# The first batch's start put in an order of its own: gated attention unit and quick-GELU layer

## The chip, the cores and the metric

The kernel runs on one core of a Trainium2 chip. A time is the device time of one execution in microseconds (us), from launch to end; times are medians over several runs. One execution was also taken by the hardware profiler; its span, the time between the first and the last instruction that the profile shows, is a little shorter than its own time. The engines are named as in the profile: PE (TensorE, matmuls), PEld (its weight loads), DVE (VectorE), ACT (ScalarE), POOL (GpSimd) and SP (SyncE, here a queue of transfers).

## The reference

For 8 batches of S = 3008 rows, with u and v of 256 columns and z of 64:

```python
scores = (1.0 / S) * np.matmul(z, z.transpose(0, 2, 1))
attn = np.maximum(scores, 0.0) ** 2
x = u * np.matmul(attn, v)                      # 24064 x 256 over all batches
h = x @ w_in                                    # w_in 256 x 2048
g = h * (1.0 / (1.0 + np.exp(-1.702 * h)))
out = g @ w_out                                 # w_out 2048 x 256
```

The score matrix of a batch is symmetric. Inputs and output are float32; the kernel computes with float16 operands and float32 sums.

## The kernel before, in words

**Tiling.** A batch's 3008 rows are NJ = 24 blocks of 128 (the last one half full), and NCH = 6 chunks of 512 (four blocks each). `ZT` holds z turned: 64 rows, held twice one below the other, and 24 x 128 columns.

**Scores.** `scores(b, group)` makes units (i, jp): the scores of the two key blocks 2jp and 2jp+1 against the 512 queries of chunk i. A unit is two matmuls of 64 rows into a pair of PSUM banks `sc` (two such pairs exist, shared with `hg`), a relu on ACT into `rl` (three buffers, L229), and a square on DVE into `a` (L243). In the first batch a unit of the upper triangle is also turned by a transfer of SP (L249) into `tt`, because the symmetric half of the matrix is not computed but taken from there. In the text, score k, relu k and square k are those of unit (0, k); score k needs the columns of z chunk k // 2.

**Attention.** `attend(b, i)` gives a list of steps; one step is one (or, in two halves, two) matmuls of a block of V by a block of squares into `o`. In the first chunk of the first batch (`both`), step n takes key block n // 2 and column half n % 2, so it needs square n // 4 and V's group n // 8. At the end, DVE multiplies `o` by u, turned before (`turn_u`, L194), into `xt`.

**First batch's z.** In later batches z is turned by a transfer. In the first, `first_z` loads z as float32 into `zf` with SP's queue, `first_cast(g)` casts chunk g twice on DVE (L123, cast g in the text), and `first_zt(g)` turns it: four transposes on PE into `zp` (L129, zp g), and a copy into ZT (L137) by ACT for g = 0 and by DVE for the others (copy ZT g). V is loaded by ACT's queue (first group) and SP's, and cast by POOL in six groups of two casts (L172). `warm_up(n)` issues n matmuls on zeros (L96), whose result is not used.

**Order.** The order of instructions on PE, POOL, SP, DVE and ACT is the program's order, written by hand. Ahead of the loop, z chunks 0 to 2 and units 0 to 2 are handled; in the loop over steps, `FIRST_ZT` says at which step of the first chunk a further z chunk is cast and turned, `SCHED0` at which steps how many units are taken (`take`), and other tables when u is turned and loaded. On DVE a ZT copy and a cast so stand in one queue with the squares. Within `take` all score matmuls of the group come ahead of its relus and squares.

**Up and down.** `up_group(b, q)` makes two blocks of 128 of the 2048 hidden columns for 512 rows: four matmuls into `hg`, the activation on ACT into `gf` (two buffers, L351), a scaling on DVE into `gt` (L352). Groups q = 0 to 7 belong to row chunk 0, 8 to 15 to chunk 1, and so on; groups 0 to 19 are spread over the steps of the last chunk's attention, and from group 20 on each is followed by one `product`. The down projection of the first four chunks is done by seven products P1 to P7 of half the size each, in place of eight; they need sums of blocks of `gt` (`left_sums`, eight DVE operations per chunk, L406 to L414) and four sums of blocks of W2 (`weight_sums`, L385 to L388, once for the whole kernel). The list `SUMS` is a queue of the former: each `up_group` takes one sum from it after its scaling. The latter are issued in the step loop, after up_group 12, 14, 16 and 18 of the first batch.

Of the kernel before, what the change touches and what calls it, by code (L numbers as in the profile page):

```python
# [11 lines left out]
P = 128  # L12
# [3 lines left out]
def kernel(  # L16
# [75 lines left out]
    def warm_up(n):  # L92

        w = ps1.tile([P, CH], F32, name="w", tag="ps1")
        for k in range(n):
            pe.matmul(w, nil[:, :P], nil, start=(k == 0), stop=(k == n - 1))  # L96
# [23 lines left out]
    def first_cast(g):  # L120
        m = g % CB * CB
        for c in range(2):
            dve.tensor_copy(ZT["st"][g // CB][:, m:m + CB, c, :], ZT["f"][g // CB][:, m:m + CB, :])  # L123

    def first_zt(g):
        z2 = ZT["st"][g // CB][:, g % CB * CB:(g % CB + 1) * CB]
        zp = ps1.tile([P, CB, P], F16, name="zp", tag="ps1")
        for k in range(CB):
            pe.transpose(zp[:, k, :], z2[:, k, :, :], ident)  # L129
        zt = ZT[0][:, g * CB:(g + 1) * CB, :].rearrange("d n p -> d (n p)")  # L130
        nb = CB if g < NCH - 1 else CB - 1
        dst = zt[:, :nb * P].rearrange("d (p n) -> d p n", n=nb)
        src = zp[:, :nb, :].rearrange("d n p -> d p n")
        if g == 0:
            act.activation(dst, src, AF.Copy, scale=1.0)
        else:
            dve.tensor_copy(dst, src)  # L137
        if nb < CB:
            dve.tensor_copy(zt[:, nb * P:], zp[:, nb, :])
# [64 lines left out]
    def folded(b, i):  # L204
        return b > 0 and i < NCH - 1

    def scores(b, group):
        scs = []
        zt = ZT[b]
        for i, jp in group:  # L210
            sc = ps2.tile([P, 2, CH], F32, name="sc", tag="ps2")
            turned = b > 0 and i < NCH - 1 and jp >= NU - 2
            kp, qi = (2 * i + jp - (NU - 2), NCH - 1) if turned else (jp, i)
            m = CB // 2 if folded(b, i) and jp == 2 * i + 1 else CB
            for r in range(2):
                h = slice(r * DQK, (r + 1) * DQK)
                pe.matmul(  # L217
                    sc[:, r, :m * P], zt[h, 2 * kp + r, :], zt[h, (qi + 1) * CB - m:(qi + 1) * CB, :],
                    start=True, stop=True,
                )  # L220
            scs.append(sc)
        for (i, jp), sc in zip(group, scs):
            rl = pw.tile([P, 2, CH], F16, name="rl", tag="rl", bufs=3)
            if folded(b, i) and jp == 2 * i + 1:
                rh = rl[:, :, :CH // 2]
                act.activation(rh, sc[:, :, :CH // 2], AF.Relu, scale=csc)
                dve.tensor_tensor(unit[b, i, jp][:, 1], rh, rh, ALU.mult)
                continue
            act.activation(rl, sc, AF.Relu, scale=csc)  # L229
            if folded(b, i) and jp == 2 * i:  # L230
                a = pa.tile([P, CB, 2, P], F16, name="a", tag="a", bufs=21)
                unit[b, i, jp] = a
                r4 = rl.rearrange("p r (q c) -> p r q c", q=CB)
                dve.tensor_tensor(a.rearrange("p q r c -> p r q c"), r4, r4, ALU.mult)
                unit[b, i, jp + 1] = pa.tile([P, 2, 2, CH // 2], F16, name="ad", tag="a", bufs=21)
                sp.dma_start_transpose(
                    unit[b, i, jp + 1][:, 0].rearrange("p g (r c) -> p (g r) c", c=P),
                    a[:, CB // 2:].rearrange("p q r c -> p (q r c)"),
                )
                continue  # L240
            a = pa.tile([P, 2, CH], F16, name="a", tag="a", bufs=21)
            unit[b, i, jp] = a
            dve.tensor_tensor(a, rl, rl, ALU.mult)  # L243
            cj = jp // 2
            if cj > i and (b or cj < NCH - 1):
                if (b, i, cj) not in TT:
                    TT[b, i, cj] = pa.tile([P, CB, CB, P], F16, name="tt", tag="tt", bufs=14)
                k0 = 2 * (jp % 2)
                sp.dma_start_transpose(  # L249
                    TT[b, i, cj][:, k0:k0 + 2].rearrange("p r g c -> p (r g) c"),  # L250
                    a.rearrange("p r c -> p (r c)"),
                )

    def weights(b, i, j):

# [80 lines left out]
    def up_group(b, q):  # L336
        k, fg = divmod(q, NFG)
        i, n = blocks(b)[k]
        hg = ps2.tile([P, FFG, CH], F32, name="hg", tag="ps2")
        for e in range(FFG):  # L340
            ff = fg * FFG + e
            for c in range(NCC):
                pe.matmul(  # L343
                    hg[:, e, :n], W1[:, c, ff * P:(ff + 1) * P], XT[b, i][:, c, :n],
                    start=(c == 0), stop=(c == NCC - 1),
                )
        if fg % 2 == 0:
            GT[b, k, fg // 2] = pa.tile([P, CB, CH], F16, name="gt", tag="tt", bufs=14)
        g = GT[b, k, fg // 2][:, (fg % 2) * FFG:(fg % 2 + 1) * FFG, :n]
        gf = pw.tile([P, FFG, CH], F32, name="gf", tag="gf")  # L350
        act.activation(gf[:, :, :n], hg[:, :, :n], AF.Gelu_apprx_sigmoid, scale=1.0 / FSC)  # L351
        dve.tensor_scalar(g, gf[:, :, :n], FSC, None, ALU.mult)  # L352
        if SUMS:
            SUMS.pop(0)()
        if k < NST and fg == NFG - 1:
            SUMS.extend(left_sums(b, k))

# [35 lines left out]
    def left_sums(b, k):  # L395
        out_ = []
        for name in ("S1", "S2", "S3", "S4"):
            for h in range(2):
                out_.append(lambda name=name, h=h: left_sum(b, k, name, h))
        return out_  # L400
# [172 lines left out]
    LOADW = {(3, NJ + 1): 0, (3, NJ + 11): 1, (4, 2): 2, (4, 10): 3, (5, 0): 4, (5, 6): 5, (5, 12): 6, (5, 18): 7}  # L573
    LOAD = {(3, NJ + 4): 4, (4, NJ + 5): 5}

    FIRST_ZT = {3: 3, 11: 4, 19: NCH - 1}
    SCHED0 = {
        0: {0: 1, 6: 2, 14: 2, 22: 2, 30: 2, 38: 2},
        1: {0: 2, 8: 2, 15: 2, 22: 2, 30: 2, 38: 2},
# [6 lines left out]
    queue = []  # L586

    def take(b, n):
        if n:
            group = [queue.pop(0) for _ in range(n)]  # L590
            scores(b, group)

    def fill(b):
        assert not queue
# [7 lines left out]
    warm_up(7)  # L602
    first_cast(0)
    first_zt(0)
    warm_up(3)
    first_cast(1)
    take(0, 2)
    first_zt(1)
    warm_up(2)
    take(0, 1)  # L610
    load_u(0, 1)
    first_cast(2)
    first_zt(2)

    for b in range(B):
        nup = NCH * NFG
        sched, turn, load = (SCHED, TURN, LOAD) if b else (SCHED0, TURN0, LOAD0)
        head = 0
        for i in range(NCH):
            for n, step in enumerate(attend(b, i, b == 0 and i < 2)):  # L620
                if b == 0 and i == 0 and n == 5:
                    load_u(0, 0)
                if b == 0 and i == 0 and n in FIRST_ZT:
                    first_cast(FIRST_ZT[n])
                    first_zt(FIRST_ZT[n])
                if (i, n) in turn:
                    turn_u(b, turn[i, n])
                if (i, n) in load:
                    load_u(b, load[i, n])
                if b == 0 and (i, n) in LOADW:  # L630
                    load_w(LOADW[i, n])
                take(b, sched[i].get(n, 0))
                if i == NCH - 1 and n >= HEAD and (n - HEAD) * LAGY // (2 * NJ - 2 - HEAD) >= head and head < LAGY:
                    up_group(b, head)
                    head += 1
                    if b == 0 and head in (13, 15, 17, 19):
                        weight_sums()[head // 2 - 6]()
                step()
        more = b + 1 < B
        if more:  # L640
            for i in range(2):
                load_u(b + 1, i)
            load_z(b + 1)
            for n0 in range(0, NJ, VB):
                load_v(b + 1, n0, sp)
            fill(b + 1)
        downs, prods = down_list(b), products()
        for q in range(head, nup):
            if more and q in (head + 14, head + 20):
                k = int(q == head + 20)  # L650
                turn_u(b + 1, k)
                load_u(b + 1, k + 2)
            up_group(b, q)
            product(b, *prods.pop(0))
        if more:
            while downs[0][0] < NCH - 2:
                down(b, *downs.pop(0))
            for k in range(NCH - 2, NCH):
                turns, steps = down64(b, k)
                at = {n: 3 - len(turns) for n in turns} | TAIL[len(turns)]  # L660
                for n, step in enumerate(steps):
                    take(b + 1, at.get(n, 0))
                    step()
        else:
            for d in downs:
                down(b, *d)
# [30 lines left out]
```

## Time and profile before

| | |
|---|---|
| median of 8 runs | 1219.36 us (1217.9 to 1220.97) |
| the profiled execution, its own time | 1218.1 us |
| its span | 1216.3 us |
| mean granted PE clock | 0.995 of full |
| PE waits for the z cast (four times) | 5.9 us |
| PE waits for the ZT copy (once) | 2.3 us |
| last V cast of the first batch ends | 17.33 us |
| score 10 (step 30 of the first chunk) starts | 29.84 us |

A row of the timeline has the start, the busy time, the engine, the line and operation, the output and the inputs with their shapes, the count, and in brackets how long the engine was idle before it and what released it. A row of the waits says who waited for whom: the total, the number of times, the longest. Rows by stretches give for each engine the busy time and the number of instructions, then the granted clock of PE as a share of full speed, the share of the DMA engines that was busy, and GB/s. Idle time of an engine that is not the bottleneck costs nothing by itself.

### The profile page before, as it was taken

What the parts mean: (1) busy time and instruction counts of PE and PEld (TensorE: products, weight loads), DVE (VectorE), ACT (ScalarE), POOL (GpSimd) and SP (SyncE); (2) the same over time, 40 slices, a digit from 0 to 9 for tenths busy, and PEclk for the clock granted to TensorE, in tenths of its full rate; (3) what the DMA queues carried; (4) which work ended last, traced back from release to release, by engine and by line L of the source; (5) the groups of instructions that cost most, each with busy time, mean ns of one, the idle gap of its engine ahead of it and who ended that gap; (6) DMA issues with size and microseconds to landing.
All of it is one profiled execution on the core that took longest, in us unless ns stands there. A gap on an engine that the chain in (4) does not pass through costs nothing.

```text
span 1216.3 us, 28032 instructions
## 1 busy us (share of the span) xinstructions
PE 1197.5 (98%) x11692; PEld 715.7 (59%) x11692; DVE 817.7 (67%) x1257; ACT 768.6 (63%) x897; POOL 306.6 (25%) x361
## 2 busy tenths in 40 slices
PE   6999999999999999999999999999999999999998
PEld 2345775557744676446764467554775547844576
DVE  4769956498554985459754697547966489564882
ACT  3777675476744768457684576836677366772763
POOL 3244410354003530034200461004520134101000
PEclk8999999999999999999999999999999999999999
DMA  9884479554794638946299553984449764496012
GB/s 216 139 137 59 156 153 168 105 114 124 144 162 99 121 110 166 152 88 154 72 174 163 87 140 92 182 145 77 135 111 184 133 85 149 116 175 116 1 36 70
DMA packets 366111, 152.32 MB, mean 125 GB/s; under 512 B 313248, under 2 KB 358048, under 8 KB 365984
## 3 DMA queue, kind: packets, MB, share of 16 engines
q1 hardware_dynamic: 328960, 113.16, 48.5%
q0 software_dynamic: 35392, 35.80, 14.6%
q8 instruction: 91, 1.49, 0.5%
q10 hardware_dynamic: 1632, 1.57, 0.4%
q14 instruction: 36, 0.29, 0.1%
HBM read 60.29 MB, written 24.64 MB: 70 GB/s over the span
## 4 chain that ended last, share of the span: by engine, by line
PE 95%; DVE 2%; DMA 2%; ACT 1%; issue 0%; ACTq 0%
PE o L302 38%; PE hg L343 26%; PE st L439 16%; PE yp L518 8%; PE sc L217 6%; DMA tt<-a 2%; PE yp L473 1%; ACT rl L229 1%; DVE gt L352 1%; PE w L96 0%; DVE a L243 0%; PE zp L129 0%; DVE s L410 0%; ACT gf L351 0%; DVE zst L123 0%
## 5 line engine op out<-in xcount | busy, mean ns | idle before, releaser
L351 ACT ACTIVATE gf<-hg 128x1024 f32<-128x1024 f32 (+1 forms) x384 | 385.6, 1007 | 167.3 <-PE hg L343 139.3
L229 ACT ACTIVATE rl<-sc 128x1024 f16<-128x1024 f32 x311 | 308.1, 1025 | 218.9 <-PE sc L217 217.0
L302 PEld LDWEIGHTS <-V 64*128 64x128 f16 (+1 forms) x4052 | 233.9, 95 | 254.1 <-issue 12.8
L343 PE MATMUL hg<-xt,W 128*128 128x512 f16 (+1 forms) x1408 | 354.6, 374 | 0.8 <-ACT gf L351 0.8
L352 DVE TENSOR_SCALAR gt<-gf 128x1024 f16<-128x1024 f32 (+1 forms) x384 | 275.4, 718 | 94.2 <-ACT gf L351 91.1
L243 DVE TENSOR_TENSOR a<-rl 128x1024 f16<-128x1024 f16 x276 | 190.8, 692 | 193.9 <-ACT rl L229 193.3
L302 PE MATMUL o<-a,V 64*128 64x512 f16 (+2 forms) x2010 | 318.2, 373 | 0.0
L187 POOL DMA_DIRECT2D uq<-in_u_dram x188 | 129.6, 696 | 519.3 <-PE sc L217 345.2
L302 PE MATMUL o<-tt,V 64*128 64x512 f16 (+1 forms) x1762 | 215.5, 376 | 3.3 <-DMA tt<-a 3.1
L343 PEld LDWEIGHTS <-W 128*128 128x128 f16 x1536 | 141.1, 98 | 118.7 <-issue 1.6
L439 PEld LDWEIGHTS <-gt 128*128 128x128 f16 x2048 | 125.1, 98 | 28.5
L217 PE MATMUL sc<-ZT 64*128 64x512 f16 (+1 forms) x692 | 122.2, 370 | 2.6 <-DVE ZT L137 2.3
L439 PEld LDWEIGHTS <-s 128*128 128x128 f16 x1536 | 93.8, 98 | 21.4 <-issue 0.6
L172 POOL CAST V<-vst 128x512 f16<-128x512 f32 x96 | 88.0, 954 | 66.9 <-DMA vst<-in_v_dram 66.8
L518 PE MATMUL yp<-W,gt 64*128 64x256 f16 x1664 | 104.0, 270 | 0.0
L518 PEld LDWEIGHTS <-gt 64*128 64x128 f16 x1664 | 80.6, 94 | 19.1 <-POOLq L84 4.1
L319 DVE TENSOR_TENSOR xt<-o,ut 128x512 f16<-128x512 f32 x80 | 51.5, 685 | 38.1 <-PE o L302 38.1
L439 PE MATMUL st<-WT,s 128*128 128x128 f16 x1024 | 67.6, 219 | 0.3 <-ACT uP L449 0.3
L439 PE MATMUL st<-WT,gt 128*128 128x128 f16 x1024 | 67.6, 219 | 0.0
L439 PE MATMUL st<-W,gt 128*128 128x128 f16 x1024 | 67.6, 219 | 0.0
L217 PEld LDWEIGHTS <-ZT 64*128 64x128 f16 x692 | 37.6, 94 | 39.8 <-issue 8.1
L152 POOL COPY zst<-zst 128x768 f16<-128x768 f16 x14 | 44.6, 3188 | 54.6 <-DMA zst<-in_z_dram 54.6
(49 smaller groups left out, 636.1 us busy)
## 6 DMA issues: line engine op xcount, KB each, us to landing
vst<-in_v_dram SPq DMA_DIRECT2D x39, 512.0 KB, 5.1
uq<-in_u_dram POOLq DMA_DIRECT2D x156, 128.0 KB, 3.3
out_dram<-y SPq DMA_DIRECT2D x32, 512.0 KB, 3.7
tt<-a SPq DMA_TRANSPOSE x230, 3.5
uq<-in_u_dram POOLq DMA_DIRECT2D x32, 112.0 KB, 3.0
out_dram<-y POOLq DMA_DIRECT2D x7, 512.0 KB, 5.1
vst<-in_v_dram SPq DMA_DIRECT2D x8, 384.0 KB, 4.7
out_dram<-y POOLq DMA_DIRECT2D x7, 384.0 KB, 5.0
```

The costliest lines, as they stand in the source:

```text
L172: pool.tensor_copy(V16[b][:, n0:n0 + VB, k, :].rearrange("p n (q c) -> p n q c", c=QW), vst.rearrange("p n (q k c) -> p n q k c", k=NCC, c ...
L187: eng.dma_start(uq[k * QW:(k + 1) * QW, :n // QW].rearrange("t q k c -> t q (k c)"), src[:, :, cs])
L217: pe.matmul(sc[:, r, :m * P], zt[h, 2 * kp + r, :], zt[h, (qi + 1) * CB - m:(qi + 1) * CB, :], start=True, stop=True,)
L229: act.activation(rl, sc, AF.Relu, scale=csc)
L243: dve.tensor_tensor(a, rl, rl, ALU.mult)
L302: ins = pe.matmul(acc[c][:, :n], V16[b][h, j, c, :], weights(b, i, j)[h], start=(k, m) == first[c], stop=(k, m) == final[c],)
L319: dve.tensor_tensor(x[:, c, :n], acc[c][:, :n], ut[:, :n], ALU.mult)
L343: pe.matmul(hg[:, e, :n], W1[:, c, ff * P:(ff + 1) * P], XT[b, i][:, c, :n], start=(c == 0), stop=(c == NCC - 1),)
L351: act.activation(gf[:, :, :n], hg[:, :, :n], AF.Gelu_apprx_sigmoid, scale=1.0 / FSC)
L352: dve.tensor_scalar(g, gf[:, :, :n], FSC, None, ALU.mult)
L439: pe.matmul(bank[:, m, :], lhs()[:, f, m, :], right[:, ff, :], start=name in ("P1", "P2", "P5") and m == 0 and ff == 0, stop=ff == NFF // ...
L518: ins = pe.matmul(yp[s // per][:, s % per, :], GT[b, k, ff // CB][h, ff % CB, s * P:(s + 1) * P], W2[h, ff, :], start=new, stop=n == last[ ...
```

## The change

- `scores` is split: it issues the score matmuls and returns one function per unit, `square`, which issues the unit's relu, square and transfer. `take` calls all of them at once, as before.
- Ahead of the loop, the matmuls of units 0 and 1 are issued, then z chunk 1 is turned, then unit 0's relu and square, the cast of chunk 2, unit 1's relu and square, and unit 2. Before, both units were complete ahead of the turn of chunk 1, and the cast and turn of chunk 2 came behind unit 2.
- The second `warm_up` has two matmuls in place of three, and the third one (two matmuls) is gone.
- Chunk 2 is now turned in the loop. The steps of the turns are 2, 7, 13 and 21 in place of (ahead of the loop), 3, 11 and 19. At each of them the turn now comes first, and behind it the cast of the next chunk.
- The four sums of W2 are appended to `SUMS` behind the eight sums of chunk 0, in place of their own places in the step loop. They are so taken by up_group 16 to 19, and the sums of each later chunk four groups later than before.

```diff
-        for (i, jp), sc in zip(group, scs):
-            rl = pw.tile([P, 2, CH], F16, name="rl", tag="rl", bufs=3)
...
+        return [lambda u_=u_, sc=sc: square(b, *u_, sc) for u_, sc in zip(group, scs)]
+
+    def square(b, i, jp, sc):
+        rl = pw.tile([P, 2, CH], F16, name="rl", tag="rl", bufs=3)
...
         if k < NST and fg == NFG - 1:
-            SUMS.extend(left_sums(b, k))
+            SUMS.extend(left_sums(b, k) + (weight_sums() if b == k == 0 else []))
...
-    FIRST_ZT = {3: 3, 11: 4, 19: NCH - 1}
+    FIRST_ZT = {2: 2, 7: 3, 13: 4, 21: NCH - 1}
...
     def take(b, n):
-        if n:
-            group = [queue.pop(0) for _ in range(n)]
-            scores(b, group)
+        for post_ in scores(b, [queue.pop(0) for _ in range(n)]):
+            post_()
...
     warm_up(7)
     first_cast(0)
     first_zt(0)
-    warm_up(3)
+    warm_up(2)
     first_cast(1)
-    take(0, 2)
+    posts = scores(0, [queue.pop(0) for _ in range(2)])
     first_zt(1)
-    warm_up(2)
+    posts[0]()
+    first_cast(2)
+    posts[1]()
     take(0, 1)
     load_u(0, 1)
-    first_cast(2)
-    first_zt(2)
...
                 if b == 0 and i == 0 and n in FIRST_ZT:
-                    first_cast(FIRST_ZT[n])
                     first_zt(FIRST_ZT[n])
+                    if FIRST_ZT[n] + 1 < NCH:
+                        first_cast(FIRST_ZT[n] + 1)
...
                     up_group(b, head)
                     head += 1
-                    if b == 0 and head in (13, 15, 17, 19):
-                        weight_sums()[head // 2 - 6]()
                 step()
```

The body of `square` is that of the old loop in `scores`, with `return` for `continue`.

More of the change, by code (lines that the diff above doesn't have):

```diff
@@ L221, in scores @@
             scs.append(sc)
-        for (i, jp), sc in zip(group, scs):
-            rl = pw.tile([P, 2, CH], F16, name="rl", tag="rl", bufs=3)
[L224 to L241, printed above, removed]
-            unit[b, i, jp] = a
[L243 to L252, printed above, removed]
@@ new lines, in scores @@
+        return [lambda u_=u_, sc=sc: square(b, *u_, sc) for u_, sc in zip(group, scs)]
+    def square(b, i, jp, sc):
+        rl = pw.tile([P, 2, CH], F16, name="rl", tag="rl", bufs=3)
+        if folded(b, i) and jp == 2 * i + 1:
+            rh = rl[:, :, :CH // 2]
+            act.activation(rh, sc[:, :, :CH // 2], AF.Relu, scale=csc)
+            dve.tensor_tensor(unit[b, i, jp][:, 1], rh, rh, ALU.mult)
+            return
+        act.activation(rl, sc, AF.Relu, scale=csc)
+        if folded(b, i) and jp == 2 * i:
+            a = pa.tile([P, CB, 2, P], F16, name="a", tag="a", bufs=21)
+            unit[b, i, jp] = a
+            r4 = rl.rearrange("p r (q c) -> p r q c", q=CB)
+            dve.tensor_tensor(a.rearrange("p q r c -> p r q c"), r4, r4, ALU.mult)
+            unit[b, i, jp + 1] = pa.tile([P, 2, 2, CH // 2], F16, name="ad", tag="a", bufs=21)
+            sp.dma_start_transpose(
+                unit[b, i, jp + 1][:, 0].rearrange("p g (r c) -> p (g r) c", c=P),
+                a[:, CB // 2:].rearrange("p q r c -> p (q r c)"),
+            )
+            return
+        a = pa.tile([P, 2, CH], F16, name="a", tag="a", bufs=21)
+        unit[b, i, jp] = a
+        dve.tensor_tensor(a, rl, rl, ALU.mult)
+        cj = jp // 2
+        if cj > i and (b or cj < NCH - 1):
+            if (b, i, cj) not in TT:
+                TT[b, i, cj] = pa.tile([P, CB, CB, P], F16, name="tt", tag="tt", bufs=14)
+            k0 = 2 * (jp % 2)
+            sp.dma_start_transpose(
+                TT[b, i, cj][:, k0:k0 + 2].rearrange("p r g c -> p (r g) c"),
+                a.rearrange("p r c -> p (r c)"),
+            )
```

## The prediction

> **What bounds the kernel now.** I read the busy times first, then TensorE's waits, then the timeline of the two places where it waits.
>
> ```profile
> PE 1197.5 (98%) x11692; PEld 715.7 (59%) x11692; DVE 817.7 (67%) x1257; ACT 768.6 (63%) x897; POOL 306.6 (25%) x361
> PEclk8999999999999999999999999999999999999999
> ```
>
> TensorE is the bound; no other engine is over 67%. Only the first slice (30 us) has a low clock. So an edit pays only where TensorE is idle or at half clock, and TensorE's own waits over the whole run are short:
>
> ```profile
> PE zp L129 <- DVE zst L123: 5.9, 4, 2.3
> PE o L302 <- DMA tt<-a: 3.1, 4, 1.4
> PE sc L217 <- DVE ZT L137: 2.3, 1, 2.3
> PE hg L343 <- ACT gf L351: 0.8, 2, 0.4
> PE st L439 <- ACT uP L449: 0.3, 1, 0.3
> ```
>
> Rows 1 and 3 (8.2 us, the three columns being total, times, longest) lie before 27 us, rows 4 and 5 between 106 and 117 us; both are places that the diff touches. Row 2 lies in later batches and is not touched. Next, the clock by stretches of 3.41 us (columns: busy time and count of PE, PEld, DVE, ACT, POOL; granted clock; DMA share; GB/s):
>
> ```profile
> 6.75:10.16 3.41, 1.11 (x10) 0.43 (x8) 1.99 (x3) 1.93 (x2) 0.89 (x2) 1.00 0.97 323
> 10.16:13.57 3.41, 1.13 (x8) 0.45 (x6) 1.16 (x4) 1.02 (x1) 2.33 (x5) 0.50 1.09 352
> 13.57:16.99 3.42, 2.50 (x10) 0.84 (x9) 1.82 (x4) 1.02 (x1) 2.33 (x5) 0.50 0.91 161
> 16.99:20.40 3.41, 3.41 (x10) 0.71 (x9) 1.21 (x2) 1.57 (x2) 2.99 (x5) 0.50 0.98 181
> 23.81:27.22 3.41, 1.64 (x12) 0.63 (x9) 2.09 (x5) 1.49 (x2) 0.00 (x0) 1.00 1.20 189
> ```
>
> The clock was full in 6.75 to 10.16, halved for the next 10.24 us, and full from 20.40 on. A stretch in which PE was busy 33% lost it, one of 48% kept it, one of 73% did not win it back, one of 100% did. At half clock a 512-column matmul takes 0.43 us, else 0.2155. The timeline shows how one turn of z waits:
>
> ```profile
> 10.65 1.02 ACT L229 ACTIVATE rl<-sc 128x1024 f16<-128x1024 f32 x1 [1.97 <-PE sc L217]
> 11.71 0.72 DVE L243 TENSOR_TENSOR a<-rl 128x1024 f16<-128x1024 f16 x1 [1.71 <-ACT rl L229]
> 12.36 0.48 DVE L123 CAST zst<-zf 128x256 f16<-128x256 f32 x2
> 12.90 0.61 PE L129 MATMUL zp<-ident,zst 128*128 128x128 f16 x4 [2.28 <-DVE zst L123]
> 13.54 0.69 DVE L137 COPY ZT<-zp 128x512 f16<-128x512 f16 x1 [0.70 <-PE zp L129]
> ```
>
> VectorE is a strict queue and idle for 1.71 us; the cast, whose z landed by about 7 us (issued by 2.6 us, 4.3 us to land), stands behind a square that waits for ScalarE, and TensorE waits 2.28 us for it. This repeats for every turn.
>
> **Part 1, the first batch's order.** I carry the queues forward in the new order, each start being the end of the one ahead or of its inputs plus 0.05 us, with these durations: four transposes or a score pair 0.2155 at full and 0.43 at half clock, ScalarE's relu 1.02 (0.91 from start to start), square 0.69 (0.60), ZT copy 0.68, two casts 0.48. Done for the old order, this puts score 10 (step 30 of the first chunk) at 29.2; the trace has 29.84, so the method is 0.6 short in 25.5.
>
> New order: zp0 at 4.4, two warm-ups instead of three to 5.7, scores 0 and 1 from 5.7, zp1 at 6.7 once cast 1 ends at 6.6. Copy ZT1 now stands ahead of square 0 and runs 7.3 to 8.0 (before 9.32 to 10.0), so score 2 starts at 8.05 instead of 10.06, score 3 at 8.3 when relu 1 frees its bank pair. Square 0 ends at 8.6: steps 0 and 1; cast 2 stands between squares 0 and 1, so zp2 at 9.1, steps 2 to 5 to 10.2. Copy ZT2 is now queued behind squares 2 and 3, which wait for relu 3 (ends 10.4): ZT2 ends 11.75, score 4 at 11.8, TensorE idle 1.6 us. Scores 4 and 5, step 6, zp3, steps 7 to 12 run to 13.95; zp4 waits for cast 4 behind squares 4 and 5 and ZT3, to 15.9, idle 1.95. From there nothing waits until score 10 at 20.9. Against 29.2 this is **8.4 us earlier**. It splits into idle time 9.3 to 5.2 (4.1), three warm-ups dropped (0.43 + 2 x 0.215 = 0.9), and 15 matmuls' worth of work at full instead of half clock (15 x 0.215 = 3.2), with 0.1 of rounding. A range for this part: 5.7 (clock lost as before) to 9.6 (before's clock stretches falling worse than in this profile).
>
> The clock decides 2.6 us of this, and dropped warm-ups speak against the change. By the rows: in my timetable PE's share of the stretches to 10.16, 13.57, 16.99 and 20.40 is 67, 53, 43 and 100% without the pipeline tails that the trace counts as busy; the old stretch to 27.22, traced at 48%, is 41% in that count, so each lies above one that kept its clock, the third barely. The Trainium skill (TensorE: Matmul & The Clock Gate, "What's actually happening") says that the clock halves after at least one idle window of about 3.4 us; the 33% stretch here lost it with no gap over 2.3 us, so row and rule differ and the row decides. By the rule nothing is lost, 8.4; if the stretch at 43% loses it, the next runs at half clock, 1.7 less.
>
> Queues past which things move: SP and POOL keep their order, only times change. SP's first two transposes go at 10.4 and 11.2 instead of 12.46 and about 16, and the four loads of u chunk 0 at about 12.5 instead of 17.21, now beside V's loads, whose last cast ended at 17.33. V's last group is needed at step 40, about 23.6, so it has 6 us, and the groups before it 4 or more. u chunk 1 is issued by POOL at 17.3 after V's casts and is turned at step 28 of the next chunk (before 44.75, then about 36.4). Transposes of squares 2 and 3 are needed at about 26.7. Nothing else has a start of its own, so the whole gain should travel to the end.
>
> Squares and casts now fall on POOL's ten V casts (0.61 each, 9.27 to 17.33). The Trainium skill (SBUF — State Buffer, "Who interferes with whom") says that a VectorE operation with two SBUF inputs shares a read interface with GpSimd, and whoever issued first holds it for a whole instruction. The rows below show both sides: a sum of 1.31 instead of 0.68 beside a copy on POOL, and a copy of 6.85 instead of 1.01 beside a full VectorE.
>
> ```profile
> 103.45 1.31 DVE L412 TENSOR_TENSOR s<-s,gt 128x1024 f16<-128x1024 f16 x1
> 111.00 6.85 POOL L152 COPY zst<-zst 128x768 f16<-128x768 f16 x1 [4.63 <-DMA zst<-in_z_dram]
> ```
>
> By the rule one holder at a time costs VectorE 0.1 us net, which my timetable holds. By the 6.85 row, V's second group, cast at 9.27, would not end before VectorE pauses at 12.4 or so; step 8 wants it at 12.9, and zp4 would slip by 1 us or less. I take the rule, and keep 1 to 3 us for the range, since a late cast comes again with each group.
>
> **Part 2, the sums of W2.** Four 0.60 us sums leave groups 12, 14, 16 and 18 and join the queue at groups 16 to 19, where they push the second block's sums four groups back.
>
> ```profile
> 105.66 0.67 DVE L406 TENSOR_TENSOR gt<-gt 128x1024 f16<-128x1024 f16 x1
> 106.26 0.68 DVE L385 TENSOR_TENSOR WT<-W 128x1024 f16<-128x1024 f16 x1
> 106.86 0.68 DVE L352 TENSOR_SCALAR gt<-gf 128x1024 f16<-128x1024 f32 x1
> 107.63 1.02 ACT L351 ACTIVATE gf<-hg 128x1024 f32<-128x1024 f32 x1 [0.77 <-DVE gt L352]
> 108.70 1.02 PE L343 MATMUL hg<-xt,W 128*128 128x512 f16 x4 [0.40 <-ACT gf L351]
> ```
>
> VectorE is full from 98.5 to 120: gt frees gf for ScalarE, whose gf frees hg's banks for TensorE. A group is 1.24 to 1.43 us on TensorE and 1.2 on VectorE with one sum, but 1.8 with two. Counted between matmul starts, TensorE loses 0.25 (106.9), 0.55 (108.7), 0.53 (111.7) and 0.44 (116.2) = 1.77 us. With one sum a group, the first stays (it comes from the slow rows at 103 to 105), the others go: gt 13 starts 0.6 earlier, and the first P6 starts at 114.67 instead of 116.20. **1.5 us**, from 0 to 1.8. The moved sums lie beside products of 1.755 us a group: groups 40 to 43, empty before, take the last four. The first consumers keep slack: P6 of block 0 is in group 21 with its W sum in 17, P6 of block 1 in group 28 with S2 in 22 and 23. Without that cover it would cost 0.6 us a sum, 2.4 in all.
>
> **Sum.** 8.4 + 1.5 = 9.9. The profiled execution took 1218.1 (span 1216.3), which gives 1208.2; the median of the runs is 1219.36, 1.3 above it, which gives **1209.5**.
>
> **Rivals.** (a) TensorE stays at half clock from 10.16 to 20.40 as before, for want of warm-ups: 2.6 us lost, 1212.1. For it: no stretch there is over 67%; against: 48% kept it. (b) VectorE and POOL hold each other up, V's groups come late: 3 us lost, 1212.5. The 6.85 row speaks for it, the undelayed casts at 124.75 (8 in 8.0 us) against. (c) Part 2 gives nothing, because POOL's copies keep VectorE late: 1211.0. (d) The saved time meets a load of fixed start (u chunk 1) and comes back whole: 1219.4; the 9 us of slack above speak against. (e) **Slower**: the clock stays half past the prologue. Every us of it costs 0.5; after (a)'s 2.6 it must last until about 40 us to eat 9.9 and 2.4 more, with PE full for six stretches, though one full stretch restored it at 20.40. About 1222.
>
> **How the numbers follow.** Likeliest 0.62, (a) 0.15, (b) 0.12, (c) 0.04, (d) 0.02, (e) 0.05. 0.2% is 2.4 us, about what a measurement can tell from no change. Faster: 0.93, same 0.02, slower 0.05. The likeliest one's own range is 1207 to 1211; to hold 8 in 10 it goes to 1214, past (a) to (c) and their sums of two.
>
> **What would show it.** Right: waits of zp on casts 4 in number before, about 2 us in one or two places after; score 10 near 21.5 (20.9 and the 0.6 that the method falls short); clock 1.00 from 6.75 on; ZT2 starting right behind square 3; no wait of hg on gf past 107 (less 8.4) and P6 with no wait on uP. Wrong: half clock after 10 us, V casts of over 1 us each, o waiting for V, or a later stage that grew between 30 and 97 us.

## The result, and the profile after

The changed kernel takes 1210.7 us (median of 11 runs, 1207.84 to 1212.22), the kernel before, in the same rounds, 1219.27 us (32 runs, 1215.54 to 1224.92). The ratio is 0.9926, with a 95% interval of 0.9916 to 0.9937: about 9 us less. The forecast was 1209.5, within 1207.0 to 1214.0. The profiled execution took 1210.7 us, its span is 1208.9 us (before 1216.3).

Busy times and granted clock by slices, changed kernel:

```profile
PE 1193.8 (99%) x11689; PEld 716.9 (59%) x11689; DVE 818.9 (68%) x1257; ACT 768.4 (64%) x897; POOL 304.6 (25%) x361
PEclk9999999999999999999999999999999999999999
```

TensorE's waits over the whole run, changed kernel (left out is the first matmul's wait for its zeros, 1.2 us as before):

```profile
PE o L304 <- DMA tt<-a: 5.0, 5, 2.0
PE sc L217 <- DVE ZT L137: 2.7, 2, 1.9
...
PE zp L129 <- DVE zst L123: 1.1, 2, 0.8
```

The waits on cast and copy of z fell from 8.2 to 3.8 us, those of hg and P6 are gone; the wait on transposes, in later batches, is 5.0 instead of 3.1. The clock by its own stretches, same kernel (the boundaries lie elsewhere than in the profile of before):

```profile
5.86:9.28 3.42, 2.34 (x19) 0.96 (x16) 2.93 (x7) 2.97 (x4) 0.57 (x1) 1.00 0.91 276
9.28:12.69 3.41, 1.47 (x10) 0.36 (x7) 3.41 (x6) 1.05 (x2) 3.41 (x5) 1.00 1.09 356
12.69:16.10 3.41, 3.36 (x13) 1.21 (x11) 2.83 (x5) 1.79 (x2) 3.33 (x5) 0.50 1.20 285
```

One stretch at half clock is left of three. It follows a stretch in which PE was busy 43%. Next, the turns of chunks 2, 3 and 4 in the timeline of the changed kernel:

```profile
8.68 2.77 DVE L245 TENSOR_TENSOR a<-rl 128x1024 f16<-128x1024 f16 x3
11.38 0.68 DVE L137 COPY ZT<-zp 128x512 f16<-128x512 f16 x1
11.98 1.27 DVE L123 CAST zst<-zf 128x256 f16<-128x256 f32 x2
12.11 0.61 PE L217 MATMUL sc<-ZT 64*128 64x512 f16 x4 [1.94 <-DVE ZT L137]
15.83 1.26 DVE L123 CAST zst<-zf 128x256 f16<-128x256 f32 x2
17.15 0.40 PE L129 MATMUL zp<-ident,zst 128*128 128x128 f16 x4 [0.80 <-DVE zst L123]
22.66 0.61 PE L217 MATMUL sc<-ZT 64*128 64x512 f16 x4
```

The same marks in the kernel before: score 10, the first up_group's matmul, and the first product with a sum of W2 (P6):

```profile
29.84 0.61 PE L217 MATMUL sc<-ZT 64*128 64x512 f16 x4
86.03 1.03 PE L343 MATMUL hg<-xt,W 128*128 128x512 f16 x4
116.20 1.05 PE L439 MATMUL st<-WT,s 128*128 128x128 f16 x16 [0.28 <-ACT uP L449]
```

In the changed kernel score 10 starts 7.18 us earlier, and the first up_group's matmul 7.17 (78.86 against 86.03): what the start of the batch (the prologue, up to score 10) had won arrives there whole. The pairs of casts of chunks 3 and 4 take 1.27 and 1.26 us, not 0.48. In the groups that follow, the changed kernel's timeline has:

```profile
98.65 1.02 ACT L353 ACTIVATE gf<-hg 128x1024 f32<-128x1024 f32 x1 [1.00 <-DVE gt L354]
99.73 1.02 PE L345 MATMUL hg<-xt,W 128*128 128x512 f16 x4
100.97 1.03 PE L345 MATMUL hg<-xt,W 128*128 128x512 f16 x4
107.50 1.06 PE L441 MATMUL st<-WT,s 128*128 128x128 f16 x16
```

The first stall stays (99.73 behind gf), then the groups follow each other every 1.24 or 1.43 us until the products join them. The first P6 (last row) is 28.64 us behind the first up_group; before it was 116.20 - 86.03 = 30.17. So the second part gave 1.53 us.

### The profile page after: what moved, and what is told of

Same layout as the page of the kernel before. It is cut to its first block, busy times and chain, and to the rows that moved or that the text cites. A ratio compares the mean times of both kernels' runs of the same rounds, so it can differ in the third digit from the quotient of the medians.

```text
span 1208.9 us, 28025 instructions
## 1 busy us (share of the span) xinstructions
PE 1193.8 (99%) x11689; PEld 716.9 (59%) x11689; DVE 818.9 (68%) x1257; ACT 768.4 (64%) x897; POOL 304.6 (25%) x361
## 4 chain that ended last, share of the span: by engine, by line
PE 95%; DMA 2%; DVE 1%; ACT 1%; issue 0%; SPq 0%; ACTq 0%
PE o L304 37%; PE hg L345 26%; PE st L441 17%; PE yp L520 8%; PE sc L217 6%; DMA tt<-a 2%; PE yp L475 1%; ACT rl L231 0%; DVE a L245 0%; DMA zf<-in_z_dram 0%; DVE gt L354 0%; DVE zst L123 0%; ACT gf L353 0%; DVE ZT L137 0%; DVE s L414 0%
## 5 line engine op out<-in xcount | busy, mean ns | idle before, releaser
L217 PEld LDWEIGHTS <-ZT 64*128 64x128 f16 x692 | 37.7, 94 | 39.2 <-issue 7.1
L194 DVE STREAM_TRANSPOSE ut<-uq 128x1024 f32<-128x1024 f32 (+1 forms) x48 | 58.3, 1215 | 0.0
```

The source lines that it names most:

```text
L194: dve.transpose(ut[:, :, :n // QW, :].rearrange("p k q t -> p q k t"), UQ.pop((b, i))[:, :n // QW])
L217: pe.matmul(sc[:, r, :m * P], zt[h, 2 * kp + r, :], zt[h, (qi + 1) * CB - m:(qi + 1) * CB, :], start=True, stop=True,)
```

## The experiments

All marks are starts on TensorE in one profile of each kernel, in us. "hg" is the first up_group, "P6" the first product with a sum of W2, "yp" the first matmul behind batch 0's products. "Waits on tt" are TensorE's waits for transposed units over the whole run. The ratio is to the kernel before in the same rounds, from 6 to 32 runs on a side.

| kernel | score 10 | hg | P6 | yp | waits on tt | span | ratio (95%) |
|---|---|---|---|---|---|---|---|
| before | 29.84 | 86.03 | 116.20 | 161.16 | 3.1 | 1216.3 | |
| changed | 22.66 | 78.86 | 107.50 | 152.46 | 5.0 | 1208.9 | 0.9926 (0.9916 to 0.9937) |
| p1_only | 22.16 | 78.36 | 108.53 | 153.49 | 2.0 | 1206.8 | 0.9953 (0.9935 to 0.9972) |
| p2_only | 29.89 | 86.09 | 114.73 | 159.68 | 4.9 | 1216.2 | 0.9993 (0.9981 to 1.0004) |
| after_warm | 24.27 | 80.46 | 109.11 | 154.06 | 1.6 | 1207.0 | 0.9933 (0.9917 to 0.9950) |
| zcast_act | 20.85 | 77.04 | 105.69 | 150.64 | 3.8 | 1206.3 | 0.9924 (0.9906 to 0.9942) |
| after_again | 24.39 | 80.58 | 109.23 | 154.19 | 3.8 | 1209.2 | 0.9919 (0.9904 to 0.9935) |
| after_third | 22.25 | 78.44 | 107.09 | 152.04 | 3.1 | 1206.6 | 0.9921 (0.9905 to 0.9937) |
| before_fill | 28.69 | 84.89 | | 160.01 | 2.6 | 1213.6 | 0.9975 (0.9967 to 0.9983) |
| hold_posts | 20.54 | 76.73 | 105.38 | 150.33 | 4.3 | 1206.3 | 0.9902 (0.9887 to 0.9917) |
| hold_posts_2 | 20.70 | 78.39 | | 151.99 | 4.1 | 1207.0 | 0.9911 (0.9890 to 0.9931) |
| hold_zact | 18.24 | | | 164.29 | 16.7 | 1218.7 | 0.9936 (0.9912 to 0.9960) |
| hold_zact_2 | 18.27 | 80.09 | | 153.69 | 8.5 | 1209.8 | one run |

### Each part alone

p1_only is the changed kernel with the sums of W2 in their old places:

```diff
-            SUMS.extend(left_sums(b, k) + (weight_sums() if b == k == 0 else []))
+            SUMS.extend(left_sums(b, k))
...
                     head += 1
+                    if b == 0 and head in (13, 15, 17, 19):
+                        weight_sums()[head // 2 - 6]()
```

> Only the new order of the prologue; the sums of W2 stay in their old places. Theory: the two parts add. Score 10 (step 30 of the first chunk) starts at about 22.7 us as in the changed kernel, 7.2 us before the old one, and TensorE still loses about 1.5 us between groups 15 and 21 (hg waiting for gf twice, P6 once). Time 7.2 us below the kernel before, 1212. Rival, that the prologue's gain is worth more in the median than in one profile: 8 us or more below, 1211 or less.

p2_only is the kernel before with the opposite edit at those two places.

> The old prologue; only the four sums of W2 join the queue of the block sums. Theory: from the first up_group to the first P6 TensorE takes 1.5 us less than before, nothing comes back in groups 20 to 47, time 1.5 us below the kernel before, 1217.8. Rival, that the later sums give it back beside GpSimd's casts: the first P6 is 1.5 us earlier but the end of batch 0's products (first yp) is not, time unchanged.

TensorE's waits in p1_only, of which the last two rows are those between groups 15 and 21:

```profile
PE hg L345 <- ACT gf L353: 0.8, 2, 0.4
PE st L441 <- ACT uP L451: 0.3, 1, 0.3
```

P6 of p2_only in the timeline:

```profile
114.73 1.06 PE L439 MATMUL st<-WT,s 128*128 128x128 f16 x16
```

From hg to P6, p1_only takes 108.53 - 78.36 = 30.17 us, as before, and p2_only 114.73 - 86.09 = 28.64, as the changed kernel: the sums are the whole of that difference, and the prologue has no share in it. From P6 to yp all four take 44.95 to 44.96 us, so nothing comes back in the groups that took the moved sums: p2_only's rival is ruled out. In the time, part 1 alone is 5.7 us below the kernel before (3.4 to 7.9), which holds the 7.2 expected and just not the rival's 8; part 2 alone is 0.9993 with an interval across 1, so its 1.5 us is shown by the profiles, not by the times. At yp, 7.67 (p1_only) and 1.48 (p2_only) are 9.15; the changed kernel has 8.70, with a score 10 that was 0.5 later in this profile. So the parts add, as near as single profiles can tell.

### The warm-ups

```diff
-    warm_up(2)
+    warm_up(3)
     first_cast(1)
...
     first_zt(1)
+    warm_up(2)
     posts[0]()
```

> The changed kernel with the warm-ups of before put back (three ahead of the cast of chunk 1, two behind the turn of chunk 1). As the prediction counted them, three warm-ups are worth 0.9 us: score 10 at 23.5, time 0.9 above the changed kernel. Rival: the first score pair is not on the path (the z transfer, cast 1 and zp1 are), so score 10 moves by 0.3 us or less and the time by as much; if the extra work keeps the clock full from 12.7 to 16.1 us, zp4 still waits for its cast, and nothing is gained by it.

after_warm puts the three warm-ups back. The time is 0.9933, with the changed kernel's 0.9919 to 0.9926 inside its interval; that interval is 4 us wide, so the times alone do not exclude 0.9 us. zp4 starts at 17.12, where three profiles of the changed kernel have 16.74, 17.15 and 17.24. So up to there the warm-ups cost nothing beyond this scatter: zp1 waits for cast 1 with or without them. Score 10 is at 24.27, but for another reason, which these stretches of after_warm show:

```profile
14.64:18.05 3.41, 1.08 (x10) 0.40 (x9) 2.83 (x5) 0.05 (x1) 3.21 (x5) 1.00 1.23 209
18.05:21.47 3.42, 3.42 (x14) 1.26 (x10) 1.98 (x5) 1.94 (x2) 2.14 (x4) 0.50 1.23 170
```

The wait ahead of zp4 left PE busy 32% of a stretch, and the next one, full of work, ran at half clock. In the changed kernel's first profile the half-clock stretch (12.69 to 16.10) ended before zp4, so its slow matmuls only shortened that wait.

### The changed kernel again

> The changed kernel once more, for its scatter beside the runs of this call. Theory: what follows the first yp is 1051.3 to 1052.1 us plus TensorE's waits on tt (1.6 to 5.0 us in six profiles, with or without the change), so the 1.9 us more that the changed kernel's profile waited there are chance; this profile has 1.6 to 5 us of them and the first yp at 152 to 153. Rival: the earlier start brings later transposes into collision: 5 us or more again.

> The changed kernel a third time: ratio to the kernel before 0.9919 to 0.9926 as in the two calls before; first yp between 152.4 and 154.2 us, by whether the clock's halved stretch falls under a wait or under full work.

These are two more measurements of the changed kernel, without an edit. The ratios are 0.9919 and 0.9921. The first yp came at 154.19 and 152.04 us, a little outside what was expected both times. The stretches of after_again around its two losses of the clock:

```profile
4.58:7.99 3.41, 1.78 (x16) 0.63 (x15) 1.87 (x4) 2.54 (x3) 1.23 (x2) 1.00 0.82 258
7.99:11.40 3.41, 3.41 (x14) 1.21 (x12) 3.31 (x6) 1.94 (x2) 2.06 (x3) 0.50 1.07 364
14.82:18.23 3.41, 1.22 (x11) 0.40 (x9) 2.92 (x5) 0.01 (x1) 3.41 (x6) 1.00 1.16 233
18.23:21.64 3.41, 3.41 (x12) 1.33 (x11) 1.93 (x5) 1.93 (x2) 1.46 (x3) 0.50 1.41 186
```

Here it lost the clock twice, after stretches with PE busy 52% and 36%; in after_third not at all after the start (score 10 at 22.25). The 52% lies above the 48% that kept the clock in the kernel before, so the busy share of a stretch alone does not decide. Between the three profiles of one program score 10 differs by 2.1 us. From zp4 to score 10, after_again takes 7.15 us and after_third 5.51: these 1.6 us are the half-clock stretch under full work. The other 0.5 lies ahead of zp4, where the copy ZT2 starts at 11.44 against 10.96, behind three squares that ended at 11.51 against 11.04.

The waits on tt: in thirteen profiles, the span behind yp, less the waits on tt that lie behind yp, is 1051.0 to 1052.2 us. For the kernel before it is 1216.33 - 161.16 - 3.1 = 1052.1, for the changed one 1208.93 - 152.46 - 5.0 = 1051.5, for after_third 1206.63 - 152.04 - 3.1 = 1051.5. So behind yp it is these waits that differ from profile to profile, and they are no larger with the change: three profiles of the same kernel had 5.0, 3.8 and 3.1, before and p2_only, with the old prologue, 3.1 and 4.9. The rival of after_again's expectation (5 us or more again) did not come.

### The clock alone

```diff
     first_zt(1)
-    warm_up(2)
+    warm_up(8)
     take(0, 1)
     load_u(0, 1)
     first_cast(2)
+    warm_up(8)
     first_zt(2)
...
                     first_cast(FIRST_ZT[n])
+                    warm_up(3)
                     first_zt(FIRST_ZT[n])
```

> The kernel before, with TensorE's idle stretches in the prologue filled with matmuls on zeros: eight in place of two behind the turn of chunk 1, eight ahead of the turn of chunk 2, three ahead of each of the later turns. It measures the clock alone. Theory: the clock stays full from the first 7 us on, and the 15 matmuls' worth of work at half clock, counted at 3.2 us in the prediction, is worth less because part of it lies ahead of waits: score 10 at about 28.1 instead of 29.84, 1.7 us. Rival: the whole 3.2, score 10 at 26.6; or nothing, if the waits swallow all of it.

before_fill is the kernel before with idle TensorE time filled. Its wait for the casts, and score 10 in its timeline:

```profile
PE zp L129 <- DVE zst L123: 4.4, 4, 1.3
```

```profile
28.69 0.61 PE L217 MATMUL sc<-ZT 64*128 64x512 f16 x4
```

The clock is full from 5.87 us to the end, and score 10 moves by 1.15 us: neither 3.2 nor nothing, and below the 1.7 expected. Four waits on the cast remain, 4.4 us, though filled in part with zeros. In the time the ratio is 0.9975 (0.9967 to 0.9983), 2.1 to 4.0 us, more than the 1.15 at score 10. The spans of the two profiles differ by 2.7; 0.5 of that is shorter waits on tt, and about 1 lies in the rest behind yp. What makes it is open. A worse clock in other executions of the kernel before does not explain it: in these rounds their mean granted clocks are 0.994 to 0.996, and the profiled execution has 0.995.

Two profiles with a full clock from the first 6 us on compare the two orders alone: before_fill has score 10 at 28.69, after_third at 22.25, so the new order is worth 6.4 us there (with the dropped warm-ups, for which after_warm shows nothing). So of the change's 7 us in the prologue the clock is a small part; the order of the queues is the rest.

### What still delays the turns: casts beside GpSimd

```diff
-            dve.tensor_copy(ZT["st"][g // CB][:, m:m + CB, c, :], ZT["f"][g // CB][:, m:m + CB, :])
+            dst, src = ZT["st"][g // CB][:, m:m + CB, c, :], ZT["f"][g // CB][:, m:m + CB, :]
+            if g < 3:
+                dve.tensor_copy(dst, src)
+            else:
+                act.activation(dst, src, AF.Copy, scale=1.0)
```

> The changed kernel with the casts of z chunks 3, 4 and 5 on ScalarE, in the same places of the order. If the missing 1.2 us of the prologue came from those casts waiting on VectorE for GpSimd's casts of V (1.27 instead of 0.48 us a pair), zp4 starts about 0.8 to 1.2 us earlier than 17.15 and score 10 at 21.5 to 21.9, time about 1 us below the changed kernel. Rival, that the squares ahead set zp4's time: zp4 at 16.9 or later, time as the changed kernel.

The timeline of zcast_act:

```profile
14.29 1.33 ACT L127 ACTIVATE zst<-zf 128x256 f16<-128x256 f32 x4
15.06 0.40 PE L133 MATMUL zp<-ident,zst 128*128 128x128 f16 x4 [0.59 <-ACT zst L127]
20.85 0.60 PE L221 MATMUL sc<-ZT 64*128 64x512 f16 x4
```

zp4 starts 2.1 us earlier and score 10 1.8 us earlier than in the changed kernel's first profile, more than expected. But the clock differs too: here it was full from 4.05 us on. Against after_third, which also had a full clock, zp4 is 1.7 and score 10 1.4 us earlier. Two things go at once: ScalarE's casts take 0.72 us beside GpSimd's, and they stand behind relu 5 instead of behind square 5 and copy ZT3. So this run shows that the cast's place on VectorE set zp4's time, and does not divide it between the two. Other profiles of the same prologue don't divide it either: in p1_only the casts of chunk 4 took 0.48 us, but squares 4 and 5 ended 0.3 us later (15.59 against 15.30), and zp4 started at 16.66; in after_third the casts took 1.27 us, and zp4 started at 16.74. In the time zcast_act (0.9924) can't be told from the changed kernel.

### The next step of the same idea

hold_posts holds relu and square of units 2 and 3 back behind ZT2 and cast 3, and those of 4 and 5 behind ZT3 and cast 4:

```diff
     posts[1]()
-    take(0, 1)
+    held = scores(0, [queue.pop(0)])
...
                     if FIRST_ZT[n] + 1 < NCH:
                         first_cast(FIRST_ZT[n] + 1)
+                    while held:
+                        held.pop(0)()
...
-                take(b, sched[i].get(n, 0))
+                if b == 0 and i == 0 and n in (0, 6):
+                    held.extend(scores(0, [queue.pop(0) for _ in range(sched[i][n])]))
+                else:
+                    take(b, sched[i].get(n, 0))
```

> The changed kernel with relu and square of units 2 and 3 held back behind the copy of ZT2 and the cast of chunk 3, and those of units 4 and 5 behind ZT3 and the cast of chunk 4. If the order on VectorE (ZT2 behind two squares that wait for ScalarE) is what still stops TensorE, score 4 starts at about 10.3 instead of 12.11, zp4 at about 13.2 instead of 17.15, score 10 at about 18.5 instead of 22.66: 4 us below the changed kernel. Rival: V's casts then set the pace (group 1 at step 8, group 2 at step 16), 1 to 2 us.

> hold_posts once more, beside the changed kernel in the same call. Theory: it is about 2 us below the changed kernel, as its first yp at 150.33 against 152.46 to 154.19 says; ratio to the kernel before about 0.990 against 0.992. Rival: the two agree within 0.5 us, because the transposes of the first batch, issued closer together, cost it back in some executions.

The timeline of hold_posts:

```profile
9.26 0.68 DVE L137 COPY ZT<-zp 128x512 f16<-128x512 f16 x1
10.00 0.61 PE L217 MATMUL sc<-ZT 64*128 64x512 f16 x4
12.90 1.26 DVE L123 CAST zst<-zf 128x256 f16<-128x256 f32 x2
14.22 0.40 PE L129 MATMUL zp<-ident,zst 128*128 128x128 f16 x4 [1.42 <-DVE zst L123]
20.54 0.61 PE L217 MATMUL sc<-ZT 64*128 64x512 f16 x4
```

ZT2 and score 4 start 2.1 us earlier than in the changed kernel's first profile, with no wait of score 4 left; zp4 starts 2.9 us earlier, and score 10 2.1, half of what was expected. Against after_third, with a full clock on both sides, score 10 is 1.7 earlier. The cast of chunk 4 is slow again (1.26). The ratios are 0.9902 and 0.9911, where the changed kernel in the same rounds has 0.9919 and 0.9921: medians of 1207.87 against 1209.41, and 1208.06 against 1209.99, so 1.5 and 1.9 us less. The intervals overlap, but both measurements agree in sign and with the 1.7 to 2.1 us of the profiles. It has the lowest ratio of all kernels here.

hold_zact is hold_posts with zcast_act's edit as well.

> As hold_posts, with the casts of z chunks 3, 4 and 5 on ScalarE too. Theory that VectorE is still the pace: another 0.5 to 1 us, score 10 at about 17.7. Rival: ScalarE is now as full as VectorE and the casts stand ahead of relus there: same as hold_posts within 0.3, or later.

> hold_zact once more for its profile. Theory: the wait of 13.7 us on a transpose at 39 us was no accident of one execution; the transposes of the first batch follow each other faster there and land late, so TensorE waits again for tt before 60 us, 3 us or more. Rival: an accident; no wait on tt before 60 us and a time near 1206.

Score 10 starts at 18.24 and 18.27, 2.3 us before hold_posts, more than expected. But the runs lie between 1206.56 and 1220.49 us, median 1212.69, ratio 0.9936, slower than hold_posts (1207.87). The timeline of hold_zact has the reason, and its stretch of 32 to 40 us the state of the DMA engines (the last column but one):

```profile
40.08 0.69 DVE L249 TENSOR_TENSOR a<-rl 128x1024 f16<-128x1024 f16 x1 [0.22 <-ACT rl L235]
52.90 1.46 PE L308 MATMUL o<-tt,V 64*128 64x512 f16 x6 [13.74 <-DMA tt<-a]
```

```profile
32.00:40.00 8.00, 7.15 (x41) 2.30 (x39) 6.66 (x10) 6.28 (x7) 2.57 (x4) 1.00 1.20 88
```

TensorE waits 13.7 us for a transposed unit of the first batch. That one was issued late rather than moved slowly; SP's queue has:

```profile
41.73 7.74 SPq L255 DMA_TRANSPOSE tt<-a  x1
49.56 1.26 SPq L255 DMA_TRANSPOSE tt<-a  x1
```

The second row is the transpose that TensorE waits for. It landed at 52.85, 3.3 us after its issue; until 49.47 the transpose ahead of it held the queue for 7.74 us, and another from 32.05 for 8.23. In the first batch of the kernel before a transpose holds SP's queue for 1.2 to 2.8 us, in the changed kernel's first profile for 1.2 to 4.6. No square ended between 40.8 and 55.9 us, so the queue was not waiting for VectorE. Landings were late as well: one took 20.4 us from its issue (before at most 7.4; 8.2, 8.4 and 10.3 in the three profiles of the changed kernel). The wait then cost more than itself: TensorE's clock fell to half from 44.0 to 57.7 us, so that 4.8 us of work behind the wait ran at half clock, an estimated 2.4 us. From score 10 to the first up_group hold_zact takes 72.45 us, hold_posts 56.19: the difference of 16.3 is the two together.

In hold_zact_2 the wait is 3.8 us, so there was a wait in both profiles. The stretch of 32 to 40 us in the kernel before, and in the changed one:

```profile
32.00:40.00 8.00, 8.00 (x43) 2.63 (x41) 6.57 (x11) 6.06 (x8) 2.57 (x4) 1.00 0.70 150
```

```profile
32.00:40.00 8.00, 8.00 (x42) 2.82 (x41) 6.18 (x9) 6.65 (x8) 0.89 (x2) 1.00 1.11 179
```

By the work done, the changed kernel's stretch answers to 39.2 to 47.2 us of the kernel before, where the share is 0.96. So the DMA engines are fuller there with the changed order (1.11; shares above 1 occur before too, 1.20 in 23.81 to 27.22), and over the whole first batch its transposes land in 6.2 us (median) instead of 3.6. hold_posts_2 already waits 1.3 us for one before 70 us, which makes up most of the 1.7 us by which its hg is behind that of hold_posts at nearly the same score 10 (0.16 later). Why single transposes hold the queue and take so much longer than others was not tried.

## Why the prediction was right, and where its sizes were off

**The bound and the two places: right.** The waits on casts and copies of z (8.2 to 3.8 us) and those of hg and P6 (to nothing) are where the time came from, and no stage between 30 and 97 us grew.

**Part 1, 8.4 us: 7.2 in the changed kernel's profile** (7.6 in after_third, 5.5 in after_again). (The two ends given, 29.2 and 20.9, differ by 8.3.) The mis-sized step is "By the rule one holder at a time costs VectorE 0.1 us net", with "two casts 0.48". The forecast had zp4 at 15.9; it came at 17.15. 0.3 us was late at ZT2 already (11.38 against 11.06 in the timetable: squares 1 to 3 took 2.77), and the pair of casts of chunk 4 took 1.26 instead of 0.48, another 0.8. In after_third ZT2 was on time (10.96), the clock was full, and zp4 came at 16.74: there the casts' 1.27 us is the whole delay. The section of the Trainium skill that the prediction named (SBUF — State Buffer, "Who interferes with whom") lists `cast`, too, among the VectorE operations that can contend with GpSimd, if their operands meet its conditions. The trace agrees with it, 1.26 us for a pair of casts beside GpSimd's casts against 0.48 away from them; no run here separates the port from another cause. The cost was set too low for two reasons. The prediction called GpSimd's casts at 124.75 undelayed, but they take 1.0 us each there, where those of the first batch take 0.61, and VectorE's operations beside them take 1.09 instead of 0.68:

```profile
124.75 8.00 POOL L172 CAST V<-vst 128x512 f16<-128x512 f32 x8 [6.90 <-DMA vst<-in_v_dram]
129.16 1.09 DVE L412 TENSOR_TENSOR s<-s,gt 128x1024 f16<-128x1024 f16 x1
```

So the profile of before already had a case of both engines working side by side, each about 0.4 us slower per operation. And V's casts did not stay where they were: ten of them ran from 9.28 to 16.95 without a pause, where before there were pauses of 0.28 to 0.80 us between the groups. The rival row, a GpSimd copy of 6.85 us, did not decide: ten casts of V took 7.67 us, and no step waited for V.

**Its split: wrong, though its sum was near.** Idle time fell by 4.4 (4.1 forecast) in the first profile, by 2.9 in after_third (waits of 5.3). The warm-ups, 0.9, were worth nothing on the way to zp4 (after_warm), because zp1 waits for cast 1 at 6.6 us either way; and the clock, 3.2, is 1.15 in before_fill's profile, because most slow matmuls stood ahead of a wait that was there anyway. Both were counted as work saved, while the path ran through VectorE: it is the new order of casts, copies and squares there, with what it moves on TensorE, that made up the gain: 6.4 us with a full clock on both sides. That the sum came near is in part luck: two terms were too high (0.9 and 3.2), and the order, of which only 4.1 us of idle time was counted, was worth more.

**The clock kept: wrong in part.** "Each lies above one that kept its clock" failed: the changed kernel's profile lost it after a stretch of 43% of busy PE, after_again after 52% and 36%, p1_only after 41%, after_warm after 32%. It cost little where it fell under a wait, and score 10 about 1.6 us where it fell under full work (after_again against after_third). Rival (a) with its three stretches did not come. The row was right against the Trainium skill's rule of an idle window (TensorE: Matmul & The Clock Gate, "What's actually happening"): in none of these was there a gap of a full stretch, the longest was 2.3 us. But the row's share of busy time is no rule either, since 52% lost the clock and 48% kept it.

**The queues: right.** V came in time; u chunk 0 was issued at 15.17, not at 12.5, because the two transposes ahead of it hold SP's queue, and no one waited for it. "Nothing else has a start of its own" held for this kernel, yet the first batch's transposes land later (6.2 us in the median instead of 3.6) and hold SP's queue longer, which the prediction did not look at; the next step of the same idea runs into it.

**Part 2, 1.5 us: right, 1.53,** with the first stall left and the others gone, and no cost where the sums went.

**The sum.** 7.18 + 1.53 = 8.7 at yp against 9.9. The profiled execution then gave back 1.3 (its span is 7.4 shorter): 1.9 more waits on tt, 0.6 less elsewhere. By the times the change is worth 9.0 us (7.7 to 10.2), and 9.6 to 9.9 in the two measurements that repeat it.

## What to carry to other kernels

On a strict queue the question for every instruction is not how long it takes but what the instruction ahead of it waits for: moving a short copy or cast ahead of work that waits for another engine won more here than the clock and the dropped work together. A list of idle, dropped and slow time that adds up to the gain is no proof of any of its terms; each needs a run that changes it alone. Where a start is brought forward, look at what else it brings forward: each transfer that it triggers meets the others sooner, and the queue that issues them may be the next bound.

## What the runs showed that was not expected

- The clock's stretches of 3.41 us have no fixed place: the first change of clock lay at 6.75, 5.86, 5.57, 5.15, 4.40 and 4.05 us in the first six profiles. In the prologues of before, the changed kernel, p1_only, p2_only and after_warm, stretches with PE busy 11, 32, 33, 36, 41, 43 and 52% lost the full clock, and one of 48% kept it; so did one of 41% in hold_posts, at 479.86 us. Three at half clock with 73 or 74% did not win it back, one of 86% and every full one did. So the share as the profile counts it does not decide alone; what does is open. One program's prologue differs by 1.6 us through this.
- Behind the first batch, thirteen profiles agree within 1.2 us once TensorE's waits on DMA transposes there (1.6 to 5.0 us) are taken off.
- Two casts of 128 x 256 from float32 on VectorE take 0.48 to 0.50 us where GpSimd's casts overlap them by 0.2 us or less, and 0.67 to 1.30 where they overlap more; on ScalarE they take 0.72 to 0.76 beside the same casts.
- Transposes by DMA in the first batch landed after up to 20.4 us instead of 3.6 (the median before) and held SP's queue for up to 8.2 us; a wait of 13.7 us on one that stood behind them, with the half clock that followed it, took back all that an earlier start had won.
